# Splitting a layer's first input through PSUM ahead of the inverse, and scaling its coefficients four units earlier

## The chip, the cores and the metric

One core of a Trainium2 chip runs the whole program. The metric is the device time of one execution in microseconds; lower is better. Engines are named as in the profile: PE (TensorE, with its weight loads as PEld), DVE (VectorE), ACT (ScalarE), POOL (GpSimd) and SP (SyncE, which here issues every DMA).

## What is computed

A decayed linear attention, and two dense layers behind it:

```
state = alpha[t] * state + k[t] v[t]^T ;  y[t] = q[t] state      (4 batches, 8 heads, 768 steps, 48 wide)
x  = y as 3072 tokens of 384
h  = x @ w_in ;  P = a0 + a1 h + a2 h^2 + a3 h^3 ;  Q = 1 + |b0||h| + |b1| h^2
x2 = (P / (Q + 1e-6)) @ w_out                                     layer 1, 2048 wide
h  = x2 @ w_in2 ;  out = (h cos h) @ w_out2                       layer 2, 2048 wide
```

## The kernel before

**Attention** is cut into 24 units (6 chunks of 128 steps by 4 batches). The loop at the end of the program runs n from -3 to 24 and calls `attention(n)`. One call issues work of several units: `scores(n)` on PE, `mask0(n)` on ACT and `mask1(n-1)` on POOL, the inverse of the decay of unit n+1 on DVE (`inverse0`, L292, and `inverse1`, L300), the scaling of q and k of unit n+1 on POOL (L311 and L306), and the state and the outputs of unit n-1 on PE. Nothing reorders: each engine runs its instructions in the order in which the program writes them.

**Weights** come as 64-bit words and are made into 32-bit floats beside the attention by `tick` and `convert`. One tile takes two ACT instructions (`words`: L68, L69), then two on DVE (L73, L74), then a rounding on ACT (`w_hi`, L205) and the remainder on POOL (`w_lo`, L217). From unit 20 on the bits between L69 and L74 of every tile lie in one and the same PSUM bank, so L69 of a tile waits until L74 of the tile before has read it. In unit 21 `turn` is [2, 1, 2, 3, 0]: L73 and L74 of a first tile ("tile A") at place 0, the words of tile B at place 1, L73 and L74 of B at place 2, all three steps of tile C at place 3.

**The layers** begin inside the attention: `layers(0)` runs after unit 20, `layers(1)` after unit 21, and so on. Numbers are kept as a rounded high part and a remainder, so a product takes three matmuls: `gemm1(n)` (L536) makes nine, over three slices kk of the input x, in the order w-hi x-hi, w-hi x-lo, w-lo x-hi. Its result lies in bank b0, b1 or b2 by n mod 3. `gemm1(0)` and `gemm1(1)` are the first two, issued in `layers(1)`. `rational(n)` then works off the results: Abs and a scaled copy on ACT (L610, L611), two steps on POOL (L612, L613), five on DVE (L602 to L618).

**The first input** x of layer 1 is loaded in units 9, 12 and 15 into the slot of x-lo. In unit 21, before, `x_hi` rounds it on ACT (L664, three times) ahead of `scores(21)`, and `x_lo` subtracts in place on DVE (L668, three times) behind the inverse of unit 22 and behind tile A's L73 and L74. Both operands and the result of L668 lie in SBUF.

**The coefficients** a and b are fetched by two tiny broadcast DMAs (L1284, L1285, tile `cab`) on SP in unit 3, and scaled by two small ACT instructions (L1287, L1288, tile `cq`) at the head of unit 6. `rational` is the only reader of `cq`.

SP issues DMAs in program order. The program gives the landings eight semaphores in turn, so an issue also waits for the landing of the issue eight before it.

Of the kernel before, what the change touches and what calls it, by code (L numbers as in the profile page):

```python
# [9 lines left out]
F32 = mybir.dt.float32  # L10
# [3 lines left out]
AF = mybir.ActivationFunctionType  # L14
ALU = mybir.AluOpType
# [6 lines left out]
NK = DM // 128  # L22
# [17 lines left out]
def attn_then_two_moe(ctx, tc, kqT, aT, vP, w1i, w1o, ma, mb, w2i, w2o, out):  # L40
    nc = tc.nc
# [57 lines left out]
    def bank(tag, shape=(128, TB), dtype=F32):  # L99

        return ps.tile(list(shape), dtype, tag=tag, name=tag)
# [31 lines left out]
    xt = {(0, 0): x_p.tile([128, 2, NK, TB], F32R, tag="x", name="x")}  # L133
    raw64 = {}
    stage = {}
    LEAD = NU - 4
# [57 lines left out]
    def early(m, s, i):  # L194

        return NF * s + i if m == 1 and NF * s + i < NF + NO else None

    def w_hi():
        while to_hi:
            m, s, i = w = to_hi.pop(0)  # L200
            at = early(m, s, i)
            hi = ws[s][i][:, 0]
            if at is not None:
                hi = kq_t[at % 3][:, 1].rearrange("p a b -> p (a b)")[:, :DM].bitcast(F32R)
            nc.scalar.activation(out=hi, in_=stage[w], func=AF.Copy)  # L205
            to_lo.append((w, hi))
# [49 lines left out]
    def parts(u):  # L256
        return [slice(0, HP // 2), slice(HP // 2, HP)] if u == 0 else [slice(0, HP)]
# [6 lines left out]
    def decay(u):  # L264
        d = U[u]
        d["p"] = in_p.tile([128, HP, C], F32, tag="p", name="p")
        a = d.pop("a")
        for h in range(HP):
            nc.vector.tensor_tensor_scan(
                d["p"][:, h], a[:, h * C:(h + 1) * C], floor([128, C]), 1.0, ALU.mult, ALU.max  # L270
            )
# [16 lines left out]
    def inverse0(u, hs):  # L288
        d = U[u]
        if hs.start == 0:  # L290
            d["m"] = temp("ah", shape=(128, HP, C))
        nc.vector.scalar_tensor_tensor(  # L292
            d["m"][:, hs], d["p"][:, hs], RANGE, d["r"][:, hs], ALU.min, ALU.mult, accum_out=sums(1, u, hs)
        )

    def inverse1(u, hs):
        d = U[u]
        if hs.start == 0:
            d["n"] = temp("z", shape=(128, HP, C))
        nc.vector.scalar_tensor_tensor(  # L300
            d["n"][:, hs], d["m"][:, hs], -2.0, d["r"][:, hs], ALU.add, ALU.mult, accum_out=sums(0, u, hs)
        )

    def scale_k(u, hs, eng):
        d = U[u]
        eng.tensor_tensor(out=d["k"][:, hs], in0=d["k"][:, hs], in1=d["n"][:, hs], op=ALU.mult)  # L306

    def scale_q(u):
        d = U[u]
        for hs in parts(u):  # L310
            nc.gpsimd.tensor_tensor(out=d["q"][:, hs], in0=d["q"][:, hs], in1=d["p"][:, hs], op=ALU.mult)  # L311

    def scores(u):
        d = U[u]
        d["sc"] = [ps_acc.tile([128, HP, C], F32, tag=f"acc{j}", name=f"sc{j}") for j in range(2)]
        for hp in range(HP):
            for j in range(2):
                js = slice(64 * j, 64 * j + D)
                nc.tensor.matmul(d["sc"][j][:, hp, :], d["k"][js, hp, :], d["q"][js, hp, :], start=True, stop=True)
# [9 lines left out]
    def mask1(u):  # L329
        for s in U[u]["s"]:  # L330
            nc.gpsimd.affine_select(
                s, s, pattern=[[0, HP], [1, C]], compare_op=ALU.is_ge, fill=0.0, base=0, channel_multiplier=-1
            )
# [7 lines left out]
    def k_out(u):  # L341
        d = U[u]
        d["kt"] = kept[u % 2]
        nc.scalar.activation(out=d["kt"], in_=d.pop("tp"), func=AF.Copy)  # L344
# [83 lines left out]
    def attention(n):  # L428

        def on(u, more=False):  # L430
            return 0 <= u < (NU - B if more else NU)

        whole = slice(0, HP)
        if on(n - 1, True):
            k_out(n - 1)
        w_hi()
        if n == LEAD + 1:
            for kk in range(NK):
                x_hi(0, 0, kk)

        if on(n):
            scores(n)

        if 0 <= n - 1 < LEAD:
            mask1(n - 1)
        at = 0 if n == -2 else n + 1
        if on(at) and n != -1:
            scale_q(at)
            if n < 1:
                for hs in parts(at):  # L450
                    inverse0(at, hs)
                    inverse1(at, hs)
                    scale_k(at, hs, nc.gpsimd)
            else:
                inverse0(n + 1, whole)
                inverse1(n + 1, whole)
                scale_k(n + 1, whole, nc.vector if n + 2 == NU else nc.gpsimd)
        convert(n, 0)
        if n == LEAD + 1:
            for kk in range(NK):  # L460
                x_lo(0, 0, kk)
        if on(n + 3):
            decay(n + 3)
        convert(n, 1)
        if on(n - 2, True):
            update1(n - 2, lambda: convert(n, 2))
        convert(n, 2)
        if on(n + 3):
            last_decay(n + 3)

        if on(n):
            mask0(n)
        if n < 0:
            guess(n + 3)
        elif n and on(n + 2):
            guess(n + 2)

        convert(n, 3)

        if on(n - 1):  # L480
            y_state(n - 1)
            y_scores(n - 1)
        if on(n - 1) and n < LEAD:
            y_out(n - 1)
        if on(n, True):
            transposes(n)
        if on(n - 1, True):
            update0(n - 1)
        convert(n, 4)
        if on(n) and n >= LEAD:  # L490
            mask1(n)
# [170 lines left out]
    def x_hi(m, blk, kk):  # L662
        x = xt[m, blk]
        nc.scalar.activation(out=x[:, 0, kk, :], in_=x[:, 1, kk, :].bitcast(F32), func=AF.Copy)  # L664

    def x_lo(m, blk, kk, eng=None):
        hi, lo = (xt[m, blk][:, i, kk, :] for i in range(2))
        (eng or nc.vector).tensor_tensor(out=lo, in0=lo.bitcast(F32), in1=hi.bitcast(F32), op=ALU.subtract)  # L668
# [521 lines left out]
    def layers(n):  # L1190
# [20 lines left out]
        if split:  # L1211
            x_hi(*nxt, at)
# [38 lines left out]
    with tc.manual_schedule():  # L1251
        nc.scalar.preload_act_table_set("natural_log_exp_and_others")
        for name, u in (("a", 0), ("kq", 0), ("a", 1), ("a", 2), ("kq", 1)):
            load(u, name)
        for t in words_t:
            nc.vector.memset(t[:, DM:DM + 1], P_MIN)
        nc.gpsimd.memset(ones, 1.0)
        nc.gpsimd.memset(half_pi, HALF_PI)
        nc.gpsimd.memset(lnb, LN_S * ONE_EPS)
        for t in v_t:  # L1260
            nc.gpsimd.memset(t[:, H * D:], 0.0)
        nc.gpsimd.memset(ident, 1.0)
        nc.gpsimd.affine_select(
            ident, ident, pattern=[[1, 128]], compare_op=ALU.is_equal, fill=0.0, base=0, channel_multiplier=-1
        )
        for s in s_all:
            nc.gpsimd.memset(s[:, HP * D:], 0.0)
        warm_up(13)
        for n in range(-3, NU + 1):
            slot[0] = n  # L1270
            if n == -1:
                load(3, "a")
                load(1, "v")
            if n >= 2:
                y_store(n - 2)
            if n >= -1:
                load(n + 5, "a")
            if n >= 0:
                load(n + 3, "kq")
                for i in range((min(n, 1) if n not in (0, 20) else 2) if n <= LEAD else 0):  # L1280
                    w_fetch(2 * NF)
                load(n + 2, "v")
            if n == 3:
                nc.sync.dma_start(out=cab[:, 0:4], in_=ma.unsqueeze(0).to_broadcast([128, 4]))  # L1284
                nc.sync.dma_start(out=cab[:, 4:6], in_=mb.unsqueeze(0).to_broadcast([128, 2]))  # L1285
            if n == 6:
                nc.scalar.activation(out=cq[:, 0:2], in_=cab[:, 4:6], func=AF.Abs)  # L1287
                nc.scalar.activation(out=cq[:, 2:6], in_=cab[:, 0:4], func=AF.Copy, scale=-LN_S * LN_S)  # L1288
            if n in X_AT:
                x_load(0, 0, X_AT.index(n))  # L1290
            if n == 1:
                warm_up(8)
            attention(n)
            if n == -3:
                for name, u in (("v", 0), ("kq", 2)):
                    load(u, name)
            w_lo(nc.gpsimd)
            if n >= LEAD:
                layers(n - LEAD)
                y_out(n - 1)  # L1300
        y_store(NU - 1)
        for n in range(NU + 1 - LEAD, F0):
            layers(n)
        for k in range(SLOTS):
            threes(k)
        acc_out()
# [178 lines left out]
```

## Time and profile before

| | |
|---|---|
| median of 3 runs | 917.72 us (916.43 to 920.28) |
| the profiled execution | 916.76 us, its span 915.0 us (1.76 us lie around the span) |
| PE, DVE, ACT, POOL busy | 98%, 77%, 76%, 78% of the span |
| granted TensorE clock, mean | 0.996 |
| DMA | 126.94 MB, 139 GB/s over the span, 322 to 385 GB/s in the first four of 40 slices |

The busy shares are means over unlike stages. PE's 98% comes from the layers, which take the last seven eighths of the span; the first eighth is attention, where the other engines and the DMAs are as full. A wait can only be worth something to the end if PE, or whatever PE waits for, is behind it.

### The profile page before, as it was taken

The numbers are of one execution on the slowest core, as the hardware profiler recorded it, in microseconds if no ns is written. First come the engines' busy times: TensorE is split into PE (matmuls) and PEld (weight loads), VectorE is DVE, ScalarE is ACT, GpSimd is POOL, SyncE is SP. The second block draws the span as 40 slices with busy tenths as digits, with TensorE's granted clock in tenths as the row PEclk, the third lists the DMA queues.
The fourth block names the chain that finished last, engine by engine and source line by source line (L and its number), as shares of the span: only waits on it lengthen the run. The fifth ranks groups of instructions, "written<-read, shape, count | busy, mean of one in ns | idle before, by whom it ended". The sixth has DMA issues, their size and how long they took to land.

```text
span 915.0 us, 15700 instructions
## 1 busy us (share of the span) xinstructions
PE 896.2 (98%) x5348; PEld 741.9 (81%) x5348; DVE 704.4 (77%) x1295; ACT 696.9 (76%) x1305; POOL 710.5 (78%) x697
## 2 busy tenths in 40 slices
PE   8899899999999999999999999999999999999996
PEld 7788667888788888888888888878888888888885
DVE  7999989989899989989979867666366554555552
ACT  6999888887879888878878878656577666666653
POOL 7999899999789989879979768759887475655332
PEclk9999999999999999999999999999999999999999
DMA  9999640100234142223156467630243432533432
GB/s 322 384 385 377 252 132 18 35 25 11 69 112 121 44 132 67 79 87 121 48 179 203 149 216 250 196 115 27 71 137 107 163 112 94 169 101 104 139 104 91
DMA packets 58120, 126.94 MB, mean 139 GB/s; under 512 B 6704, under 2 KB 19248, under 8 KB 58032
## 3 DMA queue, kind: packets, MB, share of 16 engines
q1 hardware_dynamic: 58032, 125.86, 40.7%
q8 instruction: 44, 0.72, 0.3%
q14 instruction: 44, 0.36, 0.1%
HBM read 94.37 MB, written 31.46 MB: 138 GB/s over the span
## 4 chain that ended last, share of the span: by engine, by line
PE 85%; ACT 6%; DMA 3%; issue 2%; DVE 2%; POOL 1%; SPq 0%; ACTq 0%; DVEq 0%; POOLq 0%
PE acc L552 28%; PE b L536 28%; PE acc L1016 15%; PE b L981 6%; PE r L981 5%; DMA x0d<-g 1%; PE b L1160 1%; ACT hi L326 1%; ACT r L283 1%; DMA raw<-w1i 1%; ACT g L344 1%; ACT lo L326 1%; DMA a<-aT 1%; ACT w L205 1%; ACT st L68 1%
## 5 line engine op out<-in xcount | busy, mean ns | idle before, releaser
L536 PE MATMUL b<-x,w 128*128 128x512 f32 x1143 | 289.0, 397 | 3.4 <-DVE x L668 2.4
L536 PEld LDWEIGHTS b<-x,w 128*128 128x128 f32 x1143 | 214.1, 188 | 58.0 <-DVE x L668 3.7
L552 PE MATMUL acc<-hi,w 128*128 128x512 f32 x738 | 251.5, 395 | 0.0
L587 POOL TENSOR_TENSOR lo<-g,hi 128x512 fp32r<-128x512 f32 x128 | 173.2, 1353 | 68.2 <-ACT hi L582 61.8
L552 PEld LDWEIGHTS acc<-hi,w 128*128 128x128 f32 x738 | 138.7, 188 | 33.1 <-POOL w L217 0.2
L1073 POOL TENSOR_TENSOR lo<-g,hi 128x512 fp32r<-128x512 f32 x64 | 83.1, 1299 | 103.6 <-ACT hi L1072 91.5
L552 PE MATMUL acc<-lo,w 128*128 128x512 f32 x369 | 146.2, 396 | 0.0
L582 ACT ACTIVATE hi<-g 128x512 fp32r<-128x512 f32 x128 | 80.6, 630 | 80.9 <-DVE g L618 42.3
L613 POOL TENSOR_TENSOR z<-z,ah 128x512 f32<-128x512 f32 x96 | 128.0, 1333 | 8.0
L1016 PE MATMUL acc<-hi,w_out 128*128 128x512 f32 x384 | 130.4, 395 | 0.0
L614 DVE TENSOR_TENSOR g<-g,b 128x512 f32<-128x512 f32 x96 | 65.2, 679 | 25.1 <-ACT g L611 24.5
L552 PEld LDWEIGHTS acc<-lo,w 128*128 128x128 f32 x369 | 69.4, 188 | 16.9
L612 POOL TENSOR_SCALAR z<-ah,cq 128x512 f32<-128x512 f32 x96 | 75.3, 784 | 4.4 <-ACT ah L610 4.3
L1016 PE MATMUL acc<-lo,w_out 128*128 128x512 f32 x192 | 76.4, 398 | 0.4 <-POOL lo L1073 0.2
L1016 PEld LDWEIGHTS acc<-hi,w_out 128*128 128x128 f32 x384 | 68.7, 188 | 9.9
L611 ACT ACTIVATE g<-b,cq 128x512 f32<-128x512 f32 x96 | 74.6, 777 | 0.0
L618 DVE SCALAR_TENSOR_TENSOR g<-g,cq,r 128x512 f32<-128x512 f32 x96 | 70.7, 737 | 0.1
L605 DVE SCALAR_TENSOR_TENSOR g<-g,cq,b 128x512 f32<-128x512 f32 x96 | 70.5, 735 | 0.0
L622 ACT ACTIVATE r<-z,lnb 128x512 f32<-128x512 f32 x96 | 66.7, 694 | 2.3 <-POOL z L613 2.3
L607 DVE SCALAR_TENSOR_TENSOR r<-z,r 128x512 f32<-128x512 f32 x96 | 65.4, 682 | 0.0
L602 DVE SCALAR_TENSOR_TENSOR z<-z,r 128x512 f32<-128x512 f32 x96 | 64.8, 675 | 0.0
L610 ACT ACTIVATE ah<-b 128x512 f32<-128x512 f32 x96 | 56.4, 588 | 7.3 <-PE b L536 7.1
(196 smaller groups left out, 1825.9 us busy)
## 6 DMA issues: line engine op xcount, KB each, us to landing
w_out<-wd SPq DMA_DIRECT2D x64, 384.0 KB, 3.0
kq<-kqT SPq DMA_DIRECT2D x24, 512.0 KB, 6.2
raw<-w2i SPq DMA_DIRECT2D x16, 384.0 KB, 3.5
w<-wd SPq DMA_DIRECT2D x16, 384.0 KB, 3.0
raw<-w2o SPq DMA_DIRECT2D x16, 384.0 KB, 3.2
wd<-w SPq DMA_DIRECT2D x16, 384.0 KB, 2.5
a<-aT SPq DMA_DIRECT2D x23, 256.0 KB, 5.7
x0d<-g SPq DMA_DIRECT2D x20, 256.0 KB, 5.7
```

The costliest lines, as they stand in the source:

```text
L536: nc.tensor.matmul(h, ws[0][f][:, w, ks], x[:, xx, kk, :], start=i == 0, stop=i == 8)
L552: nc.tensor.matmul(acc[k], ws[1][f][:, w, ks], d[g], start=first and i == 0, stop=last and i == 2)
L582: nc.scalar.activation(out=t["hi"], in_=t["g"], func=AF.Copy)
L587: eng.tensor_tensor(out=t["lo"], in0=t["g"], in1=t["hi"].bitcast(F32), op=ALU.subtract)
L605: nc.vector.scalar_tensor_tensor(g, g, cq[:, 3:4], two["h"], ALU.add, ALU.mult)
L611: nc.scalar.activation(out=g, in_=h, func=AF.Identity, scale=cq[:, 5:6], bias=cq[:, 4:5])
L612: nc.gpsimd.tensor_scalar(zz, ah, cq[:, 1:2], cq[:, 0:1], ALU.mult, ALU.add)
L613: nc.gpsimd.tensor_tensor(out=zz, in0=zz, in1=ah, op=ALU.mult)
L618: nc.vector.scalar_tensor_tensor(g, g, cq[:, 2:3], r, ALU.add, ALU.mult)
L981: nc.tensor.matmul(tile[:, half], w[p], x[q], start=start and i == 0, stop=True, skip_group_check=True)
L1016: nc.tensor.matmul(acc[k], item["w"][:, w, ks], item[g], start=first, stop=last)
L1073: nc.gpsimd.tensor_tensor(out=p["lo"], in0=p["g"], in1=p["hi"].bitcast(F32), op=ALU.subtract)
```

## The change

Three things. `x_split` takes the place of `x_hi` and `x_lo` in unit 21: for each slice kk ACT copies x into a PSUM bank (b1, b0, b1), ACT rounds x into the high part as before, and DVE subtracts the high part from the copy in PSUM. All of it stands at the head of the unit, ahead of `scores(21)` and ahead of the inverse of unit 22. The rounding of weights (`w_hi`) now follows it. And the DMAs of a and b move from unit 3 to unit 0, their scaling from unit 6 to unit 2.

```
@@ attention(n)
-        w_hi()
         if n == LEAD + 1:
             for kk in range(NK):
-                x_hi(0, 0, kk)
+                x_split(xt[0, 0], kk)
+        w_hi()
...
         convert(n, 0)
-        if n == LEAD + 1:
-            for kk in range(NK):
-                x_lo(0, 0, kk)
...
+    def x_split(x, kk):
+        t = bank(f"b{1 - kk % 2}")
+        hi, lo = (x[:, i, kk, :] for i in range(2))
+        nc.scalar.activation(out=t, in_=lo.bitcast(F32), func=AF.Copy)
+        nc.scalar.activation(out=hi, in_=lo.bitcast(F32), func=AF.Copy)
+        nc.vector.tensor_tensor(out=lo, in0=t, in1=hi.bitcast(F32), op=ALU.subtract)
...
-            if n == 3:
+            if n == 0:
                 nc.sync.dma_start(out=cab[:, 0:4], in_=ma.unsqueeze(0).to_broadcast([128, 4]))
                 nc.sync.dma_start(out=cab[:, 4:6], in_=mb.unsqueeze(0).to_broadcast([128, 2]))
-            if n == 6:
+            if n == 2:
                 nc.scalar.activation(out=cq[:, 0:2], in_=cab[:, 4:6], func=AF.Abs)
                 nc.scalar.activation(out=cq[:, 2:6], in_=cab[:, 0:4], func=AF.Copy, scale=-LN_S * LN_S)
```

**DVE at the head of unit 21**, before and then in the change (L363 and L365 are the state of unit 19, L292 and L300 the inverse of unit 22, L73 and L74 the tiles A, B and C, L668 the subtraction of x):

```order
L292 SCALAR_TENSOR_TENSOR ah,chk<-p,r_1769 128x512
L300 SCALAR_TENSOR_TENSOR z,chk<-ah,r_1769 128x512
L73 SCALAR_TENSOR_TENSOR b_93<-st,b_93 128x384
L74 SCALAR_TENSOR_TENSOR st<-spare,b_93 128x384
L668 TENSOR_TENSOR x<-x 128x512 x3
L363 TENSOR_TENSOR u<-s_140,u 128x192
```

```order
L668 TENSOR_TENSOR x<-b_1808,x 128x512
L668 TENSOR_TENSOR x<-b_1812,x 128x512
L668 TENSOR_TENSOR x<-b_1816,x 128x512
L292 SCALAR_TENSOR_TENSOR ah,chk<-p,r_1769 128x512
L300 SCALAR_TENSOR_TENSOR z,chk<-ah,r_1769 128x512
L73 SCALAR_TENSOR_TENSOR b_93<-st,b_93 128x384
L74 SCALAR_TENSOR_TENSOR st<-spare,b_93 128x384
L363 TENSOR_TENSOR u<-s_140,u 128x192
```

The three subtractions move ahead of the inverse and of tile A, and read a bank (b) where they read only x.

**ACT in unit 21**, before and then in the change (L405 is the output of unit 19, L326 the scores of unit 21, L283 and L284 the first guess for unit 23, L610 or L607 the Abs on the result of `gemm1(0)`):

```order
L405 ACTIVATE g<-b_1772 128x512
L664 ACTIVATE x<-x 128x512 x3
L68 ACTIVATE st<-spare 128x384
L69 ACTIVATE b_93<-spare 128x384
L326 ACTIVATE hi<-sc_1811 128x512
L326 ACTIVATE lo<-sc_1812 128x512
L283 ACTIVATE r_1842<-p 128x512
L284 ACTIVATE r_1842<-r_1842 128x512
L68 ACTIVATE st<-spare 128x384
L69 ACTIVATE b_93<-spare 128x384
L610 ACTIVATE ah<-b_1868 128x512
```

```order
L405 ACTIVATE g<-b_1772 128x512
L666 ACTIVATE b_1808<-x 128x512
L667 ACTIVATE x<-x 128x512
L666 ACTIVATE b_1812<-x 128x512
L667 ACTIVATE x<-x 128x512
L666 ACTIVATE b_1816<-x 128x512
L667 ACTIVATE x<-x 128x512
L68 ACTIVATE st<-spare 128x384
L69 ACTIVATE b_93<-spare 128x384
L326 ACTIVATE hi<-sc_1820 128x512
L326 ACTIVATE lo<-sc_1821 128x512
```

Three copies into banks are added between the roundings; what follows keeps its order (the first L68 and L69 are tile B, the second tile C).

**SP around unit 0**, before and then in the change:

```order
L243 DMA v_102<-vP 128x384
L248 DMA a<-aT 128x512
L248 DMA kq<-kqT 128x1024
L162 DMA spare<-w1i 128x768
L243 DMA v_103<-vP 128x384
```

```order
L243 DMA v_102<-vP 128x384
L1288 DMA cab<-ma 128x4
L1289 DMA cab<-mb 128x2
L248 DMA a<-aT 128x512
L248 DMA kq<-kqT 128x1024
L162 DMA spare<-w1i 128x768
L243 DMA v_103<-vP 128x384
```

The two coefficient DMAs now stand between the v of unit 2 and the a of unit 6.

## Rows read from the trace of the kernel before

**Rows 1.** Windows: us, busy us per engine (count), clock, DMA share, GB/s.

```profile
78.00:101.80 23.80, 23.27 (x374) 19.59 (x372) 22.92 (x73) 23.64 (x50) 23.80 (x28) 1.00 1.04 387
101.80:133.30 31.50, 27.02 (x226) 20.03 (x224) 27.92 (x38) 26.08 (x51) 28.04 (x27) 1.00 0.41 138
133.30:915.00 781.70, 774.73 (x3755) 641.54 (x3755) 584.42 (x966) 578.04 (x1064) 587.28 (x551) 1.00 0.33 109
```

**Rows 2.** Timeline, PE: start, us, line, operation, count [idle before, releaser].

```profile
103.81 0.50 PE L536 MATMUL b<-x,w 128*128 128x512 f32 x1
106.69 4.90 PE L536 MATMUL b<-x,w 128*128 128x512 f32 x17 [2.37 <-DVE x L668]
...
111.52 1.16 PE L319 MATMUL sc<-kq 48*128 48x128 f32 x16
...
118.09 1.16 PE L319 MATMUL sc<-kq 48*128 48x128 f32 x16 [1.07 <-POOL kq L311]
...
128.59 2.36 PE L536 MATMUL b<-x,w 128*128 128x512 f32 x9 [0.67 <-DVE g L605]
```

**Rows 3.** Timeline, DVE, head of unit 21.

```profile
100.18 0.69 DVE L292 SCALAR_TENSOR_TENSOR ah<-p,r 128x512 f32<-128x512 f32 x1 [0.19 <-ACT r L284]
...
102.59 6.12 DVE L668 TENSOR_TENSOR x<-x 128x512 fp32r<-128x512 f32 x3
...
109.48 0.55 DVE L74 SCALAR_TENSOR_TENSOR st<-spare,b 128x384 int32<-128x384 int32 x1
```

**Rows 4.** Page, part 5: a DVE group of that size with one operand in PSUM.

```profile
L614 DVE TENSOR_TENSOR g<-g,b 128x512 f32<-128x512 f32 x96 | 65.2, 679 | 25.1 <-ACT g L611 24.5
```

**Rows 5.** Timeline, POOL, the same stretch.

```profile
104.75 1.33 POOL L306 TENSOR_TENSOR kq<-kq,z 128x512 f32<-128x512 f32 x1
...
111.29 0.77 POOL L612 TENSOR_SCALAR z<-ah,cq 128x512 f32<-128x512 f32 x1 [3.12 <-ACT ah L610]
```

**Rows 6.** Timeline, ACT, the same stretch.

```profile
101.86 1.67 ACT L664 ACTIVATE x<-x 128x512 fp32r<-128x512 f32 x3
...
103.86 0.52 ACT L69 ACTIVATE b<-spare 128x384 int32<-128x384 uint8 x1
...
110.06 0.52 ACT L69 ACTIVATE b<-spare 128x384 int32<-128x384 uint8 x1 [3.12 <-DVE st L74]
110.52 0.58 ACT L610 ACTIVATE ah<-b 128x512 f32<-128x512 f32 x1
```

**Rows 7.** Tile x: line, operation, count, duration ns least/median/most, first and last start.

```profile
L664 ACT ACTIVATE x<-x x24: 616/625/632, 101.9 to 568.6; 128x512 fp32r<-128x512 f32 x24
```

**Rows 8.** Timeline, ACT, heads of units 2 and 6.

```profile
17.66 0.60 ACT L344 ACTIVATE g<-b 128x512 f32<-128x512 f32 x1
...
34.78 0.20 ACT L1287 ACTIVATE cq<-cab 128x2 f32<-128x2 f32 x1
```

**Rows 9.** Timeline, SP: the last issue ahead of the new place.

```profile
11.75 0.43 SPq L243 DMA_DIRECT2D v<-vP  x1
```

**Rows 10.** DMA issues at 11.75, 25.84, 8.50 and 14.51 us: KB, us to landing.

```profile
v<-vP SPq DMA_DIRECT2D x1, 192.0 KB, 6.2
...
cab<-mb SPq DMA_DIRECT2D x1, 1.0 KB, 6.0
...
a<-aT SPq DMA_DIRECT2D x1, 256.0 KB, 4.3
...
v<-vP SPq DMA_DIRECT2D x1, 192.0 KB, 7.7
```

**Rows 11.** Timeline, POOL, unit 3.

```profile
22.77 1.28 POOL L306 TENSOR_TENSOR kq<-kq,z 128x512 f32<-128x512 f32 x1 [0.25 <-DVE z L300]
```

**Rows 12.** Timeline, PE, at the start, and two windows behind it (columns of rows 1).

```profile
8.57 0.60 PE L319 MATMUL sc<-kq 48*128 48x128 f32 x6 [1.44 <-POOL kq L306]
...
10.00:11.00 1.00, 1.00 (x5) 1.00 (x6) 0.96 (x4) 0.97 (x2) 0.62 (x1) 0.50 1.05 399
...
13.00:14.00 1.00, 1.00 (x9) 0.88 (x10) 0.93 (x5) 0.00 (x0) 1.00 (x3) 0.84 1.02 397
```

## The prediction

> **What bounds the kernel now.** I read the windows by stage first [rows 1]. From 133.3 us to the end PE is busy for 774.73 of 781.70 us at a granted clock of 1.00, which is its upper level, 2.4 GHz: the layers are bound by PE, and nothing that the change touches lies there. So whatever the change does to the moment at which PE becomes full reaches the end one to one, and nothing else does. From 78 to 101.8 us ACT is busy 23.64 of 23.80 us, POOL 23.80 of 23.80 and the DMAs at a share of 1.04: the attention is bound by engines without gaps, so a delay put into one of them there is not made up. Between, from 101.8 to 133.3, nobody is full: PE 27.02 of 31.50, ACT 26.08, POOL 28.04. That is where the split stands.
>
> Then the timelines of that stretch. PE makes the first matmul of `gemm1(0)` at 103.81 and stands 2.37 us until the first x-lo comes from DVE [rows 2]. The three subtractions start at 102.59 and take 6.12 us [rows 3], where an operation of the same size with one operand in PSUM takes 0.679 us [rows 4], that is 2.04 us for three. The first ends when POOL's run of two-operand work ends: L306 runs from 104.75 to 106.08 [rows 5], PE goes on at 106.69. ACT then waits 3.12 us for L74 of tile B, which stands behind the subtractions, and only then makes the Abs on the result of `gemm1(0)`, at 110.52 [rows 6]. POOL waits the same 3.12 us for that Abs [rows 5] and is behind from there: scores(23) on PE wait for POOL's q at 118.09, `gemm1(5)` waits 0.67 for DVE at 128.59 [rows 2]. So the chain from 110.52 to 133 goes through ACT's Abs, POOL and DVE, and not through PE's first matmuls. This decides what the split is worth.
>
> **The split, step by step.** Removed: three copies on ACT, three subtractions on DVE with SBUF operands. Added: six ACT copies, three subtractions with a PSUM operand.
> ACT: three roundings take 1.67 us, one takes 0.625 [rows 7], so (1.67 - 0.625) / 2 = 0.52 from one to the next [rows 6]. No row here shows a 512-wide copy from SBUF to PSUM; I take 0.52 for it too. Its ends are 0.46, from the start of L69 (384 wide, into a bank) to the next start [rows 6], and 0.625, if it didn't overlap the next at all [rows 7]. The first must wait for the end of the output of unit 19 on the same bank, about 0.1. So copies and roundings run from 101.96 to 105.1 (before: to 103.4), ACT gets 1.65 us more.
> DVE: the first subtraction can start when the first rounding has ended, 101.96 + 0.52 + 0.62 = 103.1; the others follow ACT's pairs at 104.15 and 105.2. The last ends at 105.9, 2.8 us earlier than before (102.59 + 6.12 = 108.7).
> PE: `gemm1(0)` writes bank b0, which the second subtraction reads until 104.85, so it starts at 104.9 and not at 103.81, and then runs through: both take 4.2 us, to 109.1. Scores(22) could follow at 109.2, where they stood at 111.52 [rows 2]: PE has gained 2.3 us there.
> But DVE runs in order, and queued behind the waiting subtractions now are the inverse of unit 22 and L73 and L74 of tile A. Before, these four ran in DVE's idle time, from 100.18 to 102.59, 2.41 us [rows 3]. Now they run after 105.8, to 108.2. For L74 of tile A waits L69 of tile B on ACT (one bank). Before it ran at 103.86 without a wait; now it stands until 108.25. Behind it on ACT are two mask copies, the guess of unit 23 and tile C's L68: before, ACT had done these by 110.06 - 3.12 = 106.94, so from L69 on they take 106.94 - 103.86 = 3.08 us, in the shadow of the long subtraction [rows 6]. Now that cover is gone: 108.25 + 3.08 = 111.33. Tile B's L74 has by then ended (about 110.1; L69 to 108.77, then two DVE operations of 0.55 [rows 3]), so there is no second wait, and the Abs starts 0.46 later, at 111.79 against 110.52. **The split costs 1.27 us.** POOL's first step moves from 111.29 to 112.56, scores(23) from 118.09 to 119.36, and PE, which has only won a longer wait, is full 1.27 us later. Ends: -2.3 us, if the path is PE's after all, and +2.3, if the copies take 0.625 (0.3 for three), DVE's short operations run later and ACT waits a second time, for about 0.7.
> The move of `w_hi` costs nothing: no weight is waiting there in unit 21.
>
> **The coefficients, step by step.** The two scalings, 0.20 us for one [rows 8], leave unit 6 and come into unit 2: even. What is new is a wait. ACT reaches the place at 17.66 [rows 8]. SP can issue the two DMAs right behind the v of unit 2, from 11.75 + 0.43 [rows 9], at 12.2 and 12.6. The Abs is first and needs the second of them. Before, the same DMA took 6.0 us to land, and the v just ahead takes 6.2, landing at 17.95 [rows 10]. With 6.0 us it lands at 18.6; behind that v, not much before 18.0. I take 18.5: ACT waits 0.85 us. Ends: the quickest DMA near there took 4.3, so 16.9 and no wait; the slowest 7.7, so 20.3 and 2.6 us [rows 10]. Before, it landed at 31.84 for a use at 34.78: 2.9 us of cover, now gone.
> Who waits behind it: everything on ACT, which then has no gap until 106.9. POOL is no cushion: its k for unit 4 already waited 0.25 us for the inverse, which comes from ACT's guess [rows 11]. So the 0.85 stays. **The move costs 0.85 us.** The DMAs that now stand behind the two (a of unit 6, kq, a weight, v of unit 3) are issued up to 2 us later, since two of the eight places are held; that v landed only at 14.51 + 7.7 = 22.2, so an issue 2 us later still finds the queue backed up, lands no later and costs nothing.
>
> A rule speaks against that 0.85. The Trainium skill ("DMA: Bandwidth & Descriptors", Anatomy of one DMA) fits a transfer, on its GpSimd path, as about 2.0 us plus the bytes over 436 GB/s. By that estimate the coefficients would be there at 14.6, ACT would not wait, and the sum would be 1.27. Here the trace disagrees: 1 KB took 6.0 us behind a full queue [rows 10].
>
> **The sum.** 916.76 + 1.27 + 0.85 = 918.9 us, made against the profiled execution (span 915.0 and 1.76 around it). That execution lies 0.96 under the median of the three runs, 917.72, whose own spread is 3.85. For a median I put half of that offset on top: **919.4 us**, 0.2% over the median before. About 0.5%, 4.6 us, is what a measurement of this kernel can tell from no change, so this counts as the same.
>
> **The rivals.**
> *PE's path decides (faster).* If tile A's L74 or ACT's work behind it comes earlier than I have it, so that the Abs starts well before 110.52, PE's 2.3 us reach the end: 916.76 - 2.3 + 0.85 = 915.3. For it: the 2.37 us wait is real and goes. Against it: the bank that L69 shares, and 3.08 us of ACT work behind it. Chance 0.14.
> *The coefficients are there in time.* With the 4.3 us of the quickest neighbour they land at 16.9, before 17.66, and only the split is left: 918.0. The Trainium skill's page on DMA, above, would have it so. Chance 0.15.
> *PE's clock falls (slower).* In my forecast PE is done with `gemm1(2)` at about 115.2 (its bank is read by tile C's L74 until 113.05) and waits for scores(23) until 119.4, 4 us where it waited 1.07. At the start of the program, after a stop of 1.44 us and thin work around it, the clock stood at 0.50, the lower level of 1.2 GHz, from 10 us until into the window from 13 to 14, whose mean of 0.84 leaves about 0.3 us of it: some 3.3 us [rows 12]. After the 2.37 us at 104 it did not fall [rows 1, 2]. If it falls here for as long, PE loses 3.3 / 2 = 1.65 us, of which its later wait of 0.67 swallows a part: 918.9 + 1.0 = 919.9. With the coefficients at their late end as well, 2.6 for 0.85, it is 921.7. What decides is whether the clock stays up through that stop. The Trainium skill ("TensorE: Matmul & The Clock Gate", HAM oscillation) says that waits between bursts of matmuls put the clock back to half. No run here shows a gap as long as this one. Chance 0.13.
>
> **How the numbers follow.** The forecast itself gets 0.53, the three rivals 0.14, 0.15 and 0.13, and 0.05 is left for what I don't see. The range goes from 914.8, the fast rival less half a microsecond, to 922.5, the slow one with the late landing and the offset to the median. Faster by over 0.5% would need nearly all of PE's idle time between 104 and 133, 4.5 us: 0.02. Slower by over 0.5% needs the slow rival and the late landing together, or a second ACT wait: 0.07. Within: 0.91.
>
> **What would show it.** Right: L668 at about 0.68 us each and no PE wait on it; an ACT wait of nearly 3 us moved from tile C's L69 to tile B's, for DVE's L74; the Abs on `gemm1(0)` some 9.8 us behind ACT's first step on x, where it was 110.52 - 101.86 = 8.7; a PE wait of some 4 us before scores(23); an ACT wait before the first coefficient scaling. Wrong: an Abs that comes closer to that step than before, or scalings that start without a wait.

## The result: 0.66% slower, and the profile after

| | before | after |
|---|---|---|
| median | 916.99 us (6 runs, 916.26 to 920.28) | 923.72 us (6 runs, 920.99 to 924.46) |
| profiled execution, its span | 916.76, 915.0 us | 923.56, 921.8 us |

The ratio is 1.0066, with a 95% interval of 1.0050 to 1.0083. The forecast, 919.4 with 914.8 to 922.5, is too low, and so is the upper end of its range. In the profiles the span is 6.8 us longer.

Read in order of time. ACT at the head of units 1 and 2 (start, us, line, operation, [idle before, releaser]):

```profile
14.00 0.60 ACT L326 ACTIVATE hi<-sc 128x512 f32<-128x512 f32 x1 [1.38 <-PE sc L319]
...
16.11 0.59 ACT L405 ACTIVATE g<-b 128x512 f32<-128x512 f32 x1
20.09 0.20 ACT L1291 ACTIVATE cq<-cab 128x2 f32<-128x2 f32 x1 [3.39 <-DMA cab<-mb]
20.20 0.19 ACT L1292 ACTIVATE cq<-cab 128x4 f32<-128x4 f32 x1
20.29 0.58 ACT L344 ACTIVATE g<-b 128x512 f32<-128x512 f32 x1
```

The wait that the forecast put at 0.85 us is 3.39. ACT's L344 stood at 17.66 before [rows 8] and stands at 20.29 now, 2.63 later. SP issues the two DMAs where the forecast had them:

```profile
12.19 0.53 SPq L1288 DMA_DIRECT2D cab<-ma  x1
12.76 0.58 SPq L1289 DMA_DIRECT2D cab<-mb  x1
```

The second takes 7.3 us to land, where the same DMA took 6.0 [rows 10], and lands at 12.76 + 7.3 = 20.06:

```profile
cab<-mb SPq DMA_DIRECT2D x1, 1.0 KB, 7.3
```

And between 16 and 20 us the DMAs nearly stop. Windows of half a microsecond and then of the four (columns as in rows 1: the last three are clock, DMA share, GB/s), and the four in the kernel before:

```profile
16.50:17.00 0.50, 0.50 (x9) 0.50 (x10) 0.47 (x3) 0.20 (x1) 0.50 (x2) 1.00 0.45 158
17.00:17.50 0.50, 0.50 (x12) 0.42 (x8) 0.50 (x1) 0.00 (x0) 0.50 (x1) 1.00 0.21 63
17.50:18.00 0.50, 0.50 (x10) 0.46 (x9) 0.50 (x4) 0.00 (x0) 0.50 (x2) 1.00 0.04 1
18.00:18.50 0.50, 0.50 (x13) 0.47 (x9) 0.50 (x2) 0.00 (x0) 0.50 (x1) 1.00 0.22 67
...
16.00:20.00 4.00, 2.52 (x42) 2.03 (x38) 2.66 (x8) 0.70 (x2) 4.00 (x5) 1.00 0.53 193
```

```profile
16.00:20.00 4.00, 3.96 (x58) 3.21 (x56) 2.81 (x10) 3.97 (x10) 4.00 (x5) 1.00 1.01 373
```

A share of 0.53 over 4 us, where it was 1.01, is 1.9 us of DMA time lost. Then ACT stands twice more, at 76.94 for a store that is late (0.54 us) and at 91.08 for PE (0.96 us), and reaches x at 106.11 where it was 101.86 [rows 6]: 4.25 later.

The split itself, DVE and ACT:

```profile
107.29 0.69 DVE L668 TENSOR_TENSOR x<-b,x 128x512 fp32r<-128x512 f32 x1 [3.16 <-ACT x L667]
...
111.91 0.55 DVE L74 SCALAR_TENSOR_TENSOR st<-spare,b 128x384 int32<-128x384 int32 x1
```

```profile
112.49 0.51 ACT L69 ACTIVATE b<-spare 128x384 int32<-128x384 uint8 x1 [2.72 <-DVE st L74]
...
115.90 0.59 ACT L607 ACTIVATE ah<-b 128x512 f32<-128x512 f32 x1
```

The subtractions take 0.69 us each where three took 6.12 [rows 3], and ACT waits for tile A's L74 on tile B's L69. The Abs comes 115.90 - 106.11 = 9.79 us after ACT's first step on x (before 8.66).

Then PE, and the clock behind its wait:

```profile
109.08 4.46 PE L533 MATMUL b<-x,w 128*128 128x512 f32 x18 [1.05 <-DVE x L668]
...
117.21 2.36 PE L533 MATMUL b<-x,w 128*128 128x512 f32 x9
...
123.44 1.44 PE L319 MATMUL sc<-kq 48*128 48x128 f32 x16 [3.86 <-POOL kq L311]
...
128.62 3.42 PE L533 MATMUL b<-x,w 128*128 128x512 f32 x9
```

```profile
121.00:124.00 3.00, 0.56 (x10) 0.56 (x12) 2.05 (x4) 2.97 (x7) 3.00 (x4) 1.00 0.00 0
124.00:127.00 3.00, 3.00 (x32) 2.44 (x30) 3.00 (x5) 2.60 (x6) 2.92 (x4) 0.53 0.63 202
127.00:130.00 3.00, 3.00 (x19) 2.45 (x17) 2.19 (x4) 2.48 (x6) 2.92 (x5) 0.50 0.85 271
130.00:133.00 3.00, 3.00 (x25) 2.13 (x23) 1.82 (x2) 2.59 (x6) 3.00 (x3) 0.83 0.73 225
```

PE stands 3.86 us for POOL's q, where it stood 1.07 [rows 2]. Right behind, the granted clock is at its lower level, 1.2 GHz (0.50), into the window from 130 us on (0.83), and nine matmuls take 3.42 us where they take 2.36 at the upper one. In rows 1 this stage had 1.00.

The 6.8 us of span are therefore 4.25 up to x, 1.13 from x to the Abs, and 1.4 from the Abs to the end (804.5 us before, 805.9 now). This compares one profile with one; the kernel before was profiled twice more, below, and there the first two parts come out differently.

### The profile page after: what moved, and what is told of

The parts are those of the page before. It is cut to its first block, busy times and chain, and to the rows that moved or that the text cites. A ratio compares the mean times of both kernels' runs of the same rounds, so it can differ in the third digit from the quotient of the medians.

```text
span 921.8 us, 15703 instructions
## 1 busy us (share of the span) xinstructions
PE 899.0 (98%) x5348; PEld 745.1 (81%) x5348; DVE 702.6 (76%) x1295; ACT 698.5 (76%) x1308; POOL 709.1 (77%) x697
## 4 chain that ended last, share of the span: by engine, by line
PE 88%; DMA 4%; ACT 3%; DVE 2%; POOL 1%; issue 1%; SPq 0%; ACTq 0%; DVEq 0%; POOLq 0%
PE b L533 28%; PE acc L549 28%; PE acc L1020 15%; PE b L985 6%; PE r L985 5%; DMA a<-aT 1%; PE sc L319 1%; PE b L1164 1%; DMA kq<-kqT 1%; DMA cab<-mb 1%; DMA v<-vP 1%; PE b L394 1%; DVE p L269 1%; PE u L351 1%; POOL w L217 0%
## 5 line engine op out<-in xcount | busy, mean ns | idle before, releaser
L610 POOL TENSOR_TENSOR z<-z,ah 128x512 f32<-128x512 f32 x96 | 126.9, 1322 | 8.0
L607 ACT ACTIVATE ah<-b 128x512 f32<-128x512 f32 x96 | 56.5, 588 | 7.8 <-PE b L533 7.4
```

Of the source, the lines that this page charges most:

```text
L610: nc.gpsimd.tensor_tensor(out=zz, in0=zz, in1=ah, op=ALU.mult)
```

## The experiments

Theory A: the wait of ACT for the coefficients is what costs, since ACT has no gap in the attention that could take it up; the rest is the place of the split and PE's clock. Rivals: it is the DMAs that stand late behind the two tiny ones (B); the split in its new place is what costs (C).

**The coefficients alone.**

```
before.py
-            if n == 3:
+            if n == 0:
                 nc.sync.dma_start(out=cab[:, 0:4], in_=ma.unsqueeze(0).to_broadcast([128, 4]))
...
-            if n == 6:
+            if n == 2:
                 nc.scalar.activation(out=cq[:, 0:2], in_=cab[:, 4:6], func=AF.Abs)
```

> The kernel before with only the coefficients moved (DMAs in unit 0, scaling in unit 2), x split as before. Theory A (ACT stands for the coefficients, and the tiny DMAs hold up the queue for the loads behind them): an ACT wait of 3 us or more ahead of the first scaling, small waits for late loads further on, and 3.5 to 4.5 us over the kernel before. Rival B (the split and PE's clock make up the whole loss, and the attention absorbs the wait): within 1 us of the kernel before.

Measured: 921.52 us against 917.51, ratio 1.0044 (1.0030 to 1.0058): +4.0 us.

```profile
20.60 0.20 ACT L1287 ACTIVATE cq<-cab 128x2 f32<-128x2 f32 x1 [3.99 <-DMA cab<-mb]
...
104.75 1.67 ACT L664 ACTIVATE x<-x 128x512 fp32r<-128x512 f32 x3
```

The wait is there without the split, and between 20.60 and 104.75 us ACT waits for nothing else: the small waits for late loads that were expected further on didn't come. This move is most of the loss.

**The split alone.**

```
before.py, attention(n); x_split is defined as in the change
-        w_hi()
         if n == LEAD + 1:
             for kk in range(NK):
-                x_hi(0, 0, kk)
+                x_split(xt[0, 0], kk)
+        w_hi()
...
         convert(n, 0)
-        if n == LEAD + 1:
-            for kk in range(NK):
-                x_lo(0, 0, kk)
```

> The kernel before with only the split changed (copies in PSUM, subtractions ahead of the inverse), coefficients as before. Theory A: ACT's first step on x to the Abs of the first product takes 9.8 us (8.7 before), so 1.2 us lost, and PE's stop before the scores of unit 23 grows to some 4 us; if its clock falls there, 1.5 to 2 us more, 3 us over the kernel before in all. Without the fall 1.2 us over it. Rival B, that the split alone makes the loss: 5 us or more. Rival C, that PE's earlier first products are worth something: under the kernel before.

Measured: 918.58 against 917.51, ratio 1.0008 (0.9999 to 1.0017): +1.1 us by the medians, which is hardly clear of nothing. The clock fell, and yet the 3 us expected with it didn't come. Again 9.79 us from x to the Abs (104.60 to 114.39), a stop before scores(23), and a clock of 0.66 from 121 to 126 us:

```profile
121.91 1.48 PE L319 MATMUL sc<-kq 48*128 48x128 f32 x16 [3.86 <-POOL kq L311]
```

The profiled execution took 922.06 us, 3.5 over the median: ahead of x ACT waited 3.1 us in sum for late stores.

**The DMAs early, their use late.**

```
before.py
-            if n == 3:
+            if n == 0:
                 nc.sync.dma_start(out=cab[:, 0:4], in_=ma.unsqueeze(0).to_broadcast([128, 4]))
```

> The kernel before with the two coefficient DMAs in unit 0 and the scaling left in unit 6. Theory A1 (what costs is that ACT waits for them): no wait ahead of the scaling, the stop of the DMAs near 17 us stays, and the time lies within 1.5 us of the kernel before. Theory A2 (what costs is that the DMAs stop, since the attention lives on them): 3 to 4 us over it, as with the scaling in unit 2.

Measured: 918.41 against 917.51, ratio 1.0014 (1.0001 to 1.0027).

```profile
16.00:20.00 4.00, 3.42 (x57) 2.77 (x52) 3.82 (x12) 3.97 (x10) 4.00 (x6) 1.00 0.53 196
```

This is the same stop as in the change, but ACT doesn't wait at the scaling. So of the 4.0 us the stopped queue costs about 1, and ACT's wait the rest: B falls as the main cause.

**A delay of ACT with no DMA in it.**

```
before.py; idle is a new tile of 128x128
+            if n == 2:
+                for i in range(12):
+                    nc.scalar.activation(out=idle, in_=ident, func=AF.Copy)
```

> The kernel before, with twelve extra ACT copies of a 128x128 constant into a tile that nobody reads, at the head of unit 2; the coefficients and the split as before. It prices an ACT delay alone: no DMA is added or moved there, nothing waits for a landing. The twelve should take about 2.4 us (0.20 us for a small one). Theory 1 (ACT and POOL have no gap from unit 2 to unit 21, so a delay of ACT is not made up): the first ACT step on x moves by about 2.4 us and the median rises by 2.2 to 2.6 us. Rival (the cost of the move comes from the DMAs that are late, and ACT's wait is made up in the attention): the first step on x moves by under 0.8 us and the median rises by under 1.

Measured: 922.41 against 917.25, ratio 1.0060 (1.0047 to 1.0073). The twelve took 21.80 - 17.83 = 3.97 us, 0.33 each and not 0.20:

```profile
17.83 4.06 ACT L1289 ACTIVATE idle<-ident 128x128 f32<-128x128 f32 x12
21.80 0.58 ACT L345 ACTIVATE g<-b 128x512 f32<-128x512 f32 x1
...
105.93 1.66 ACT L665 ACTIVATE x<-x 128x512 fp32r<-128x512 f32 x3
```

So 3.97 us of delay at 18 us arrive as 4.07 at x (105.93 against 101.86, where ACT had stood for PE at the head as long as here, 2.33 and 2.42 us): nothing is made up over 84 us. A holds, with one reserve: the run isn't free of late DMAs. SP stands 4.8 us for the store of an ACT result that is now late, and the DMA share is 0.39 from 24 to 28 us. But from 21.80 to 105.93 us ACT waits for nothing, so what arrives is ACT's own delay. The median rose by 5.2, about 1 more, and the profile shows where: x to the Abs takes 115.49 - 105.93 = 9.56 us, against the 8.66 of the first profile. That difference is there without a delay too (below).

**The split behind the inverse**: `x_split` at the old place of `x_lo`, the coefficients as before.

```
before.py, attention(n); x_split is defined as in the change
-        if n == LEAD + 1:
-            for kk in range(NK):
-                x_hi(0, 0, kk)
...
         convert(n, 0)
         if n == LEAD + 1:
             for kk in range(NK):
-                x_lo(0, 0, kk)
+                x_split(xt[0, 0], kk)
```

> The kernel before with the split through PSUM, but its subtractions left behind the inverse and the first weight tile; coefficients as before. ACT's order is that of the change. Theory A (the loss of the split is the place of the subtractions on DVE, the PSUM copy itself gains): no long wait of ACT for the weight tile, ACT's first step on x to the Abs of the first product in about 7.2 us instead of 8.7, and 1 to 2 us under the kernel before. Rival (the three more ACT copies are what costs): 9.8 us to the Abs, 1 us or more over it.

Measured: 914.76 against 917.51, ratio 0.9969 (0.9958 to 0.9980). **It beats both kernels.** The short subtractions stay, L69 no longer waits for L74, and the Abs comes 108.92 - 101.95 = 6.97 us after the first step on x:

```profile
101.95 0.60 ACT L666 ACTIVATE b<-x 128x512 f32<-128x512 f32 x1
...
105.53 0.51 ACT L69 ACTIVATE b<-spare 128x384 int32<-128x384 uint8 x1
...
108.92 0.58 ACT L607 ACTIVATE ah<-b 128x512 f32<-128x512 f32 x1
```

It gains 2.8 us where 1 to 2 were expected. So it is the queueing of the inverse and of tile A behind the subtractions that spoils the split, not PSUM and not the three copies.

**Both moves, the split behind the inverse.**

```
after.py, attention(n)
-        if n == LEAD + 1:
-            for kk in range(NK):
-                x_split(xt[0, 0], kk)
         w_hi()
...
         convert(n, 0)
+        if n == LEAD + 1:
+            for kk in range(NK):
+                x_split(xt[0, 0], kk)
```

> The changed kernel with one thing different: the split through PSUM stands behind the inverse and tile A, where the subtractions were before; the coefficients stay in units 0 and 2. If the place of the split and the move of the coefficients are separate costs: the coefficients' 4.0 us as measured alone, less the 2.8 us that the split behind gains alone, so 918.8 us, and 4 to 5 us under the changed kernel; the Abs about 7.0 us behind ACT's first step on x; the clock at 1.00. If they are not (the late attention eats the gain, or the coefficients alone cost so much because of the old split's wait): above 920.5 or below 917.

Measured: 918.30 against 917.25, ratio 1.0009 (1.0000 to 1.0019), and 5.4 us under the changed kernel. X to the Abs takes 6.96 us again, and the wait is there:

```profile
21.60 0.20 ACT L1291 ACTIVATE cq<-cab 128x2 f32<-128x2 f32 x1 [3.22 <-DMA cab<-mb]
```

In this execution (920.71 us) PE's clock had fallen at the head and ACT stood 2.59 us there, so that it reached the scaling as late as 18.4. It waited 3.22 us all the same, since the second DMA, issued at 13.27, took 8.3 us to land.

Against the split behind alone the coefficients cost 918.30 - 914.76 = 3.5 us. The clock fell once more, to 0.53 from 124 to 127 us, against what was expected, but not at the cost of the end (below).

**PE kept busy before scores(23)**, in the changed kernel:

```
after.py, scores(n)
+        if u == LEAD + 3:
+            for i in range(14):
+                nc.tensor.matmul(d["sc"][0][:, i % HP, :], ident, ident, start=True, stop=True)
```

> The changed kernel, with fourteen extra 128x128 matmuls of a constant into the bank of the scores of unit 23, ahead of those scores, which overwrite it. They fill a part of the wait of 3.86 us in which PE stands for POOL's q. If the fall of PE's clock behind that wait is what makes the end move by more than the 5.4 us by which the Abs had moved: the granted clock stays at 1.00 from 121 to 133 us, the nine matmuls of the fourth product take 2.4 us in place of 3.42, and the median falls by 1.0 to 1.8 us, to about 922. If the fall doesn't matter or comes all the same: a median within 0.5 us of the changed kernel's.

Measured: 921.58 against 917.25, ratio 1.0049 (1.0034 to 1.0063). The trace counts 28 matmuls for the fourteen.

```profile
117.31 3.39 PE L318 MATMUL sc<-ident 128*128 128x128 f32 x28
121.35 1.16 PE L322 MATMUL sc<-kq 48*128 48x128 f32 x16 [0.65 <-POOL kq L311]
...
124.48 2.36 PE L536 MATMUL b<-x,w 128*128 128x512 f32 x9
```

The clock is 1.00 in every window from 101 to 133 us. Scores(23) still wait for POOL, 0.65 us, and the program behind them is that of the changed kernel. From the Abs to the end are 918.2 - 113.78 = 804.4 us, as in the kernel before; the changed kernel needs 805.9. The clock is worth 1.5 us by the two profiles. Their spans differ by 3.6; the other 2.1 arise ahead of x, which this run reached at 103.99. The medians differ by 2.1, a little more than was expected, and the two intervals overlap, so the price of the clock rests on the profiles.

**The coefficients late**, in the kernel with the split behind the inverse.

```
split behind the inverse
-            if n == 3:
+            if n == 17:
                 nc.sync.dma_start(out=cab[:, 0:4], in_=ma.unsqueeze(0).to_broadcast([128, 4]))
...
-            if n == 6:
+            if n == LEAD + 1:
                 nc.scalar.activation(out=cq[:, 0:2], in_=cab[:, 4:6], func=AF.Abs)
```

> The kernel with the split behind the inverse, and the coefficients fetched in unit 17 and scaled at the head of unit 21, in place of units 3 and 6. If the two tiny DMAs stop the queue by themselves, wherever they stand in a full stream, the DMA share falls for half a microsecond to two around their landing here too, and the median is the same as without this move (914.8) within 0.5 us, or up to 1 us higher if a load of x or a store comes late by it; ACT has no wait at the scaling. If the stop belongs to the first units alone (a full queue of large loads), no such dip is seen, and the median falls by up to 0.5 us.

Measured: 915.29, ratio 0.9976 (0.9966 to 0.9987): not better than with units 3 and 6. No wait at the scaling, landings of 4.8 and 5.6 us, and only a shallow dip (a DMA share of 0.83 from 92 to 94 us).

**How the queue stops.** The same kernel with the scaling in unit 6, first with the two DMAs apart, then with both at n == 1 (not printed).

```
split behind the inverse
-            if n == 3:
+            if n == 0:
                 nc.sync.dma_start(out=cab[:, 0:4], in_=ma.unsqueeze(0).to_broadcast([128, 4]))
+            if n == 2:
                 nc.sync.dma_start(out=cab[:, 4:6], in_=mb.unsqueeze(0).to_broadcast([128, 2]))
```

> The kernel with the split behind the inverse, the DMA of a in unit 0, that of b in unit 2, the scaling left in unit 6. In unit 0 the two stand 0.5 us apart on SP and the DMA share is near nothing for about 2 us; in units 3 and 17 they stood 0.9 to 1.0 us apart and the dip was a quarter of that or less. If two tiny broadcasts close behind one another make the long stop: one alone leaves a dip of half a microsecond at most around 17 to 19 us, share from 16 to 20 us above 0.85. If one tiny broadcast in that place is enough: share from 16 to 20 us at 0.6 to 0.8, a stop of a microsecond. Median within 1 us of 914.8 in both.

> The same, with both DMAs in unit 1, the scaling in unit 6. If what counts is the place in the program (only behind the first loads, where the queue is longest): a smaller dip, as in unit 3, about 0.5 us lost, median 914.8 within 0.7 us. If they stop the queue as in unit 0 wherever SP issues them close together: 1.5 to 2 us lost in the stretch from 18 to 26 us, landings of 6.8 us and more, and a median 0.5 to 1.5 us above 914.8.

Measured: 915.50 (0.9981, 0.9970 to 0.9993) and 915.65 (0.9976, 0.9965 to 0.9986).

```profile
16.00:20.00 4.00, 4.00 (x68) 3.48 (x66) 2.44 (x9) 3.97 (x9) 3.93 (x5) 1.00 0.66 250
20.00:24.00 4.00, 3.21 (x54) 2.62 (x51) 3.92 (x13) 3.97 (x10) 3.35 (x4) 1.00 1.04 406
```

This is the first of the two: one tiny broadcast alone, in unit 0, costs 0.34 x 4 = 1.4 us of DMA time. So two that stand close together are not needed for it. In the second the share is 0.72 from 20 to 24 us, 1.1 us lost, with landings of 6.6 and 7.0 us: between the two sizes that were expected. Neither shows a cost in the median that could be told from 914.76.

**The kernel before, profiled twice more.**

> The kernel before, unchanged, profiled once more. In the one profile that the forecast was made from, PE's clock had fallen at 10 to 13 us and ACT stood 2.42 us there, and from ACT's first step on x to the Abs were 8.66 us; in three other kernels with the old split ACT stood 1.39 us or less at that place where the clock had not fallen, and the old split took 9.56 to 10.06. If that profile was the ordinary case: an ACT wait of about 2.4 us at 12 to 16 us, the first step on x near 101.9, 8.6 to 8.8 us to the Abs. If it was the exception in both: a wait of 1.4, the first step on x near 101, 9.5 to 10.1 us to the Abs, so that the split in its new place costs nothing by its length, and what it costs is PE's clock alone.

> The same kernel once more, to see which of the two is the more frequent: an ACT wait of 2.4 us at the head and 8.7 us from the first step on x to the Abs, or 1.4 and 9.5 to 10.1.

Measured: 916.81 and 917.32 us (one run each). ACT's wait at the head is 1.39 and 1.38 us, not 2.42:

```profile
14.05 0.60 ACT L326 ACTIVATE hi<-sc 128x512 f32<-128x512 f32 x1 [1.39 <-PE sc L319]
...
102.04 1.66 ACT L664 ACTIVATE x<-x 128x512 fp32r<-128x512 f32 x3
...
111.03 0.60 ACT L610 ACTIVATE ah<-b 128x512 f32<-128x512 f32 x1
```

From x to the Abs are 8.99 here and 9.94 in the third (101.39 to 111.33), after 8.66 in the first. The three other kernels with the old split took 9.56 (ACT delayed), 9.69 (DMAs early) and 10.06 (coefficients alone). So 8.66 is the shortest of six, whose middle is 9.6. The first profile stands alone in one more thing: only there did PE's clock stay up behind the stop for the first x-lo, 2.37 us [rows 2]. In the five others that stop is 3.04 to 3.66 us and the clock is 0.50 for 3 to 7 us behind it. The third profile (PE, a window, ACT):

```profile
107.52 6.79 PE L536 MATMUL b<-x,w 128*128 128x512 f32 x17 [3.63 <-DVE x L668]
...
107.00:113.00 6.00, 5.48 (x13) 4.33 (x14) 4.71 (x10) 2.19 (x5) 0.79 (x2) 0.50 0.01 3
...
111.33 0.60 ACT L610 ACTIVATE ah<-b 128x512 f32<-128x512 f32 x1 [0.79 <-PE b L536]
```

In those five the subtractions take 6.38 to 6.72 us (6.12 in the first), ACT waits 3.39 to 3.72 us for L74 (3.12), and in four of them the Abs waits another 0.35 to 0.79 us for PE. The fall at the head [rows 12] is another matter: with it ACT stood 1.82 to 2.59 us there in five of the fourteen profiles, without it 1.38 or 1.39 in nine. The two don't go together: the kernel with ACT delayed, which the expectation counts among those without the fall, had it, with 2.33 us, and still took 9.56.

## Why the prediction was wrong

**The step that failed is the term for the coefficients**: 0.85 us, with an upper end of 2.6. It measured 4.0 us alone and 3.5 beside the better split. Three parts of it were off.

- ACT's arrival. The forecast took 17.66 from the one profile [rows 8], in which the clock had fallen at 10 to 13 us [rows 12] and ACT had stood 2.42 us for PE. Without that fall ACT is there at 16.11 + 0.48 = 16.6. That is 1.1 us. The forecast even quoted this fall for its slow rival and did not see that it also sets the 17.66. How far this part stands by itself is not shown: in the kernel with both moves ACT came late, at 18.4, and the landing was late with it.
- The landing. The forecast took 18.5, and it came at about 20.06 (12.76 + 7.3). The two DMAs stop the queue that they stand in: that is 1.6 us, and 0.85 + 1.1 + 1.6 is the 3.4 to 3.5 us seen. The late end, 7.7 us from the slowest neighbour [rows 10], is about what came (6.7 to 8.3 in the five profiles with both DMAs in unit 0; 7.3 in this one); in this profile it was the combination with an earlier ACT that lay outside the range.
- "Lands no later and costs nothing" for the DMAs behind the two. The kernel with the DMAs early and the use late says about 1 us (1.3 by the ratio, between 0.1 and 2.5).

That ACT's delay stays, since ACT is without gaps, was right, and the delay of ACT alone shows it: 3.97 in, 4.07 out.

The rival that the coefficients are there in time falls, and with it the estimate from the Trainium skill ("DMA: Bandwidth & Descriptors", Anatomy of one DMA): the page's fit, made for its GpSimd path, has a fixed 2 us and the bytes, which would have had them there at 14.6. They landed at 20.06.

**The split's steps came as forecast; that its size did too is luck.** The subtractions took 0.69 us (0.68 forecast), ACT's pairs 1.04 (0.52 + 0.52), tile B's L69 waited 2.72 (nearly 3), the Abs came after 9.79 us (9.8), PE waited 3.86 (some 4). One sign failed as it was worded: PE did wait for L668, 1.05 us, which is what the forecast's own step has (104.9 against 103.81). The size, 1.1 us for 1.27, agrees because two errors cancel. The 1.27 was taken against 8.66, the shortest of six; against their middle, 9.6, the 9.79 of the new place cost 0.2. And PE's clock, which the forecast left out of its likeliest case, costs 1.5. Their sum, 1.7, is a little above what the interval of the split alone allows (-0.1 to 1.6). The same middle fits the split behind the inverse: 9.6 - 6.97 = 2.7 us, and its median is 2.8 lower.

**The rival that PE's clock falls came true**, at 1.5 us for the 1.0 given, in both kernels that have the split ahead and nothing in PE's stop. Span less the start of the Abs is 805.9 and 806.0 us in those two and 804.1 to 804.8 in the twelve other profiles, the one with PE kept busy among them. But PE's clock falls ahead of the Abs in two of the three profiles of the kernel before, and in five of the six with the old split; in the change it is 1.00 there: the split moves the fall. The sentence "after the 2.37 us at 104 it did not fall" was true of the one profile alone. The Trainium skill's rule ("TensorE: Matmul & The Clock Gate", HAM oscillation), that waits between bursts of matmuls put the clock back, agrees with this trace: 0.53 and 0.50 behind the 3.86 us. With the late landing this rival gave 921.7, the nearest of the forecasts; its chance of 0.13 was too small, since the wait of 4 us before scores(23) stood in the forecast itself and a wait of 1.44 had already been followed by a fall [rows 12].

**PE's path decides** falls: measured from ACT's first step on x, PE was released 1.9 us earlier (2.97 us after it, before 4.83 [rows 2, 6]) and waited for POOL's q all the more.

The parts don't add up without a rest. 4.0 and 1.1 are 5.1; the change costs 6.1 to 6.7, as the base is taken. The rest of 1.0 to 1.6 us stays open. In single profiles ACT's waits for late stores before x vary from none to 3.1 us in sum, so one profile can't place it.

## What to carry to other kernels

Where an engine runs without gaps, as ACT does here, a wait put into it early comes out at the end, so a load should be used where it has landed with some cover, not as soon as it is expected: unit 6 had 2.9 us of cover, and unit 21 was no better. A step that is made shorter should not also be moved ahead of what others wait for: the same subtractions in their old place gave 0.3%, and in the new place nothing. Take the times on which a small difference rests from more than one profile: here both bases, ACT's arrival at 17.66 and the 8.66 us from x to the Abs, came from an execution that the two others of the same kernel don't repeat.

## What was not expected of the hardware

**A tiny broadcast stops a full queue.** The 2 KB and 1 KB DMAs (128 rows of 16 and 8 bytes) in unit 0 take the DMA share from 1.01 to between 0.49 and 0.55 for 4 us in five kernels, with 1 GB/s in the worst half microsecond of the change. The loads were there to be moved: in the change the two behind the tiny ones were issued at 13.44 and 14.15 us and landed at 20.7 and 22.8. In unit 1 the tiny ones lose 1.1 us; in unit 3 of the kernel before about 0.5; in unit 17 some 0.3. Landings go roughly the same way: 6.2 to 8.3 us in unit 0, 6.6 and 7.0 in unit 1, 4.9 to 7.2 in unit 3, 4.8 and 5.6 in unit 17. Why the early ones are worse stays open.

**PE's clock and the length of a stop.** In the kernel before, a stop of 2.37 us left the clock at 1.00 [rows 1, 2]. In its two other profiles stops of 3.50 and 3.63 at the same place went with 0.95 and 0.89 over the stage, and stops of 3.04 to 3.66 in the three other kernels with the old split were followed by 0.50 too. But in the five kernels with the split behind, a stop of 1.65 to 1.69 us before scores(23), with many small matmuls after it, was followed by a fall in four and by none in the fifth, and two of them read:

```profile
117.31 1.16 PE L319 MATMUL sc<-kq 48*128 48x128 f32 x16 [1.69 <-POOL kq L311]
...
121.69 2.68 PE L533 MATMUL b<-x,w 128*128 128x512 f32 x9
126.35 4.47 PE L533 MATMUL b<-x,w 128*128 128x512 f32 x18
```

```profile
117.58 1.16 PE L319 MATMUL sc<-kq 48*128 48x128 f32 x16 [1.66 <-POOL kq L311]
...
125.05 2.37 PE L533 MATMUL b<-x,w 128*128 128x512 f32 x9
128.07 2.36 PE L533 MATMUL b<-x,w 128*128 128x512 f32 x9 [0.65 <-DVE g L602]
```

The first (coefficients late) lost time to the lower clock and then had no wait for DVE; the second (DMAs apart) kept the clock and waited 0.65 us. From the Abs to the end they need 804.5 and 804.6 us. In the change the clock also falls behind ACT's wait for the coefficients, to 0.50 from 24 to 28 us, where ACT is busy 3.97 of 4.00 us and doesn't wait for PE. So in these runs a fall of the clock costs only what the next wait doesn't swallow, and the length of a stop alone doesn't tell whether it falls.

**A copy into PSUM is no dearer on ACT.** L666, 512 wide from SBUF to PSUM, takes 0.58 to 0.60 us, the rounding behind it from SBUF to SBUF 0.61, with 0.52 from start to start.
